# Reordering the first part and the loop of a planned attention and maxout kernel, and holding batch 3's loads behind w_out

## The chip, the cores and the metric

The kernel runs on one core of one Trainium2 chip. The metric is the device time of one execution in microseconds (us), as the median of several runs. All times below are us unless marked ns.

## The reference

`x` is 8 batches x 8 heads x 512 positions x 64, `state` 8 x 8 x 32 x 64. Per batch and head:

```
a     = softmax(x state^T / 8)          # 512 x 32
xread = a state                         # 512 x 64
a2    = softmax(state x^T / 8)          # 32 x 512
sread = a2 x                            # 32 x 64
```

The rows of `xread` and `sread` of a batch, heads side by side, are 544 rows of 512 numbers, 4352 rows in all. On each row `r` runs a maxout layer and an output layer:

```
h   = max(r w1, r w2, r w3)             # w1, w2, w3: 512 x 768
out = h w_out                           # w_out: 768 x 512
```

Inputs and output are float32.

## The kernel before

The kernel computes in bf16. GpSimd's (POOL's) DMAs convert on the way, so w1 to w3, w_out and nearly all of x come as bf16; the first half of batch 0's x and the states come as float32 over the queues of SyncE (SP) and ScalarE (ACT), and an engine casts them.

The products of `xread` with w1, w2 and w3 are not formed from `xread`. Since `xread = a state`, the kernel multiplies the states by the weights first: `G = state W` per batch (32 x 8 heads = 256 rows, 3 x 768 columns), and layer 1 is then `a G`, with only 256 instead of 512 terms to sum.

The whole work is a list of named steps in three texts, `FIRST` (lines 18 to 39: the loads, batches 0 and 1, the beginning of 2), `EACH` (lines 40 to 47: run five times, for batch b = 2 to 6, numbers in it are relative to b) and `LAST` (lines 48 to 64: batch 7, the `sread` rows of all batches, and the last stores). `perform` (line 543) calls the functions of the steps in the order of the text, and each engine and each queue then runs its own share strictly in that order, waiting where an operand isn't there. So the text is the schedule. Beside it stand `BANKS` and `PAIRS`: one digit for each request for a PSUM bank (four single banks, 0 to 3) or for a pair of banks (two pairs). A bank is written anew when its last holder has been copied out.

The steps, with the engine that does them; a last letter gives the engine or queue (D = VectorE or DVE, A = ACT, P = POOL, S = SP; two letters share the work in halves):

- `lst k`: load the states of batches 2k and 2k+1; `lxu`, `lxg b g`: load one half of batch b's heads (uncast over SP, cast over POOL); `lx b`: a whole batch over POOL; `lw m0 m1 i`: load columns m0*128 to m1*128 of w1, w2 or w3 (i = 0, 1, 2) over POOL; `lwo`: w_out over POOL. POOL has eight semaphores for its DMAs, and the ninth waits for the first to land.
- `cxu`: cast the half that came uncast. `stc k`, `stt k`, `stp k`: cast the states, turn them on TensorE (PE, line 221), place them as block matrices. `clr`, `zero`, `ident`, `xones`: constants. `warm`: load the exponential's table.
- `xt b g`, `xtc b g`: turn half of x on PE (line 236) and copy it out (line 243); `xtd b`: the same for a whole batch by a DMA transpose on SP (line 248).
- `sc`: scores on PE (line 261); `ex`: exponential on ACT (line 268); `sum`: row sums and their reciprocal on DVE (lines 275 and 277); `wt`: the product that gives `a` (line 283); `at`, `atc` or, by DMA on SP, `atd`: turn `a` (lines 294, 297, 301).
- `pad b`: POOL copies x with a column of ones beside it, 2 copies (line 310); `sr b`: `sread` on PE (line 326; for batches 0 and 1 straight from x, for the others from pad's copy); `srs`: divide it on DVE (lines 336 to 342); `srt`: turn it by a DMA on SP (line 345); `ap`: put it in place.
- `g b m`, `gc b m`: one slice of G, 128 columns of each of w1 to w3, on PE (line 362) and its copy (line 380); `gr b c0 c1`, `grc`: a run of columns of G (lines 362, 402, 405).
- `l1 b m`: layer 1 for 128 hidden columns, six matmuls into three banks (line 415); `m0`, `ma`, `mb`: the first bank is copied by ACT (line 430), DVE takes the maximum with the second (line 435) and the third (line 439).
- `l2 b j`: layer 2 for a quarter of the batch's rows, six matmuls (line 446); `l2c`: copy out (line 453); `so`: store (line 476).
- `busy n`: n matmuls on zeros (line 210) that fill PE where nothing is ready. `ones`: POOL sets a constant that only the last part reads (line 194).

In `FIRST` before, batches 0 and 1 go side by side: both softmaxes stand ahead of the first layer-1 step, POOL loads x of batch 1 first, then x of batch 0, then W in nine pieces of 128 to 384 columns, the last two behind batch 1's softmax products, then w_out and batch 3's x.

Of the kernel before, what the change touches and what calls it, by code (L numbers as in the profile page):

```python
# [15 lines left out]


FIRST = """
    lxu 0 0 S; lst 0 A; lxg 1 0; zero; warm; clr 0; clr 1; clr 2; clr 3; stc 0 D; ident; busy 1;
    lst 1 S; busy 2; busy 1; busy 2; busy 1; busy 1; stt 0; busy 1; busy 2; cxu 0 0 D; stp 0 AD;  # L20
    stc 1 A; lxg 0 1; xt 0 0; lxg 1 1; lw 0 1 0; busy 1; lw 0 3 1; xtc 0 0 A; xt 1 0; xones 0; busy 2;
    busy 1; lw 0 2 2; xtc 1 0 DA; sc 0 0; xt 0 1; lw 1 2 0; busy 1; busy 1; lw 2 4 0; lw 2 4 2; sc 1 0;
    ex 0 0; ex 1 0; busy 1; xtc 0 1 A; xt 1 1; busy 1; busy 1; sum 0 0; busy 1; stt 1; lw 3 6 1; busy 1;
    sc 0 1; busy 1; ex 0 1; xtc 1 1 D; busy 1; sc 1 1; ex 1 1; busy 1; stp 1 A; lxg 2 1; wt 0 0 P;
    busy 1; xones 1; at 0 0; sum 1 0; busy 1; busy 1; sum 0 1; sr 0; busy 1; sum 1 1; g 0 0; wt 1 0 P;
    g 1 0; gc 1 0 A; wt 0 1 D; sr 1; busy 1; srs 0; lxg 2 0; at 0 1; at 1 0; wt 1 1 P; atc 0 0 D;
    at 1 1; gc 0 0 D; atc 0 1 A; lw 4 6 2; srs 1; atc 1 0 A; g 1 1; atc 1 1 D; gc 1 1 A; g 0 1;
    l1 0 0 1; g 1 2; m0 0 0; g 0 2; l1 1 0; gc 0 1 D; gc 1 2 A; l1 1 1; m0 1 0; ma 0 0; mb 0 0; ma 1 0;
    lw 4 6 0; mb 1 0; l1 0 1; g 0 3; m0 1 1; g 1 3; gc 0 2 A; l1 0 2; ma 1 1; l1 1 2; xtd 2; pad 2;
    m0 0 1; mb 1 1; ma 0 1; m0 0 2; lst 3 A; gc 0 3 DA; l1 0 3; m0 1 2; lwo; gc 1 3 A; ones; g 0 5;  # L30
    g 1 4; mb 0 1; ma 0 2; lxg 3 0; m0 0 3; mb 0 2; gc 0 5 A; lst 2 S; ma 1 2; l1 1 3; stc 3 P; m0 1 3;
    l1 0 5; mb 1 2; g 0 4; gc 1 4 A; g 1 5; ma 0 3; l1 1 4; m0 0 5; gc 0 4 A; mb 0 3; ma 1 3; m0 1 4;
    lxg 3 1; l1 0 4; sc 2 -; gc 1 5 A; xtd 3; mb 1 3; gr 2 1024 1280; m0 0 4; gr 2 1280 1792; ex 2 -;
    grc 2 1280 1792 A; l1 1 5; m0 1 5; ma 0 5; stc 2 A; mb 0 5; gr 2 512 1024; gr 2 1792 2304; sr 2;
    ma 1 4; mb 1 4; ma 0 4; mb 0 4; l2 0 3; grc 2 512 1024 A; stt 2; grc 2 1024 1280 D; gr 2 0 512;
    l2 0 0; l2 0 1; l2 0 2; grc 2 1792 2304 A; sum 2 -; l2c 0 0 A; grc 2 0 512 A; ma 1 5; wt 2 - P;
    srs 2; l2c 0 3 A; stp 2 A; mb 1 5; l2c 0 2 D; atd 2; so 0 2 4 P; stt 3; l2c 0 1 A; stp 3 DA;
    so 0 0 2 A; lx 4;
# [638 lines left out]
```

## Time and profile before

| what | value |
|---|---|
| median of 3 runs | 153.15 (153.15 to 153.26) |
| the profiled execution | 153.01 |
| its span, first to last instruction | 151.2 |
| instructions | 3644 |
| HBM read, written | 15.20 MB, 8.91 MB |
| granted TensorE clock over the span | 0.999 of full |

The span is what the profile's times count from and to; 1.8 lie around it. The page gives busy time by engine, the chain of work that ended last, and groups of instructions by source line; the trace behind it can be asked for the instructions of one engine in order of time (start, duration, engine, line, operation, what is written and read, shapes, how many of the same kind in a row, and in brackets how long the engine stood idle before and what ended that), for single DMAs with the time from issue to landing, and for busy time in windows. Matmuls are pipelined, so the step from one start to the next is a matmul's price and its printed duration is longer.

### The profile page before, as it was taken

What the parts mean: (1) busy time and instruction counts of PE and PEld (TensorE: products, weight loads), DVE (VectorE), ACT (ScalarE), POOL (GpSimd) and SP (SyncE); (2) the same over time, 40 slices, a digit from 0 to 9 for tenths busy, and PEclk for the clock granted to TensorE, in tenths of its full rate; (3) what the DMA queues carried; (4) which work ended last, traced back from release to release, by engine and by line L of the source; (5) the groups of instructions that cost most, each with busy time, mean ns of one, the idle gap of its engine ahead of it and who ended that gap; (6) DMA issues with size and microseconds to landing.
All of it is one profiled execution on the core that took longest, in us unless ns stands there. A gap on an engine that the chain in (4) does not pass through costs nothing.

```text
span 151.2 us, 3644 instructions
## 1 busy us (share of the span) xinstructions
PE 146.6 (97%) x1434; PEld 73.6 (49%) x1434; DVE 115.1 (76%) x202; ACT 85.4 (56%) x147; POOL 54.7 (36%) x74
## 2 busy tenths in 40 slices
PE   6999999999999999999999999999999999999992
PEld 2465444344444443444354435443544445679771
DVE  6458899889168799879986998798879887675353
ACT  3567866779677671767175817581758353331220
POOL 6998518301336505460456054604260100001500
PEclk9999999999999999999999999999999999999999
DMA  3999999994919979998199829982133110300545
GB/s 112 241 193 195 198 196 203 161 197 59 204 53 262 225 89 269 152 193 182 60 168 228 174 94 163 206 176 80 72 139 87 68 79 7 131 8 17 188 170 198
DMA packets 38581, 22.30 MB, mean 147 GB/s; under 512 B 22032, under 2 KB 36368, under 8 KB 38560
## 3 DMA queue, kind: packets, MB, share of 16 engines
q0 software_dynamic: 15200, 13.44, 46.6%
q1 hardware_dynamic: 21920, 6.95, 23.5%
q10 hardware_dynamic: 1440, 1.64, 3.2%
q8 instruction: 12, 0.20, 0.5%
q14 instruction: 9, 0.07, 0.2%
HBM read 15.20 MB, written 8.91 MB: 159 GB/s over the span
## 4 chain that ended last, share of the span: by engine, by line
PE 92%; DMA 4%; issue 1%; POOL 1%; DVE 1%; POOLq 0%
PE pw L415 47%; PE po L446 25%; PE pg L362 6%; PE po L461 4%; DMA x<-in_x_dram 4%; PE psr L326 2%; PE ps L261 2%; PE idle L210 2%; PE pgh L362 1%; PE pat L294 1%; POOL x L169 1%; DVE held L521 0%; PE pt L221 0%; PE pxt L236 0%; PE idle L519 0%
## 5 line engine op out<-in xcount | busy, mean ns | idle before, releaser
L415 PE MATMUL pw<-aT,G 128*128 128x512 bf16 x288 | 66.6, 379 | 0.0
L430 ACT CAST t<-pw 128x512 bf16<-128x512 f32 (+1 forms) x54 | 30.4, 563 | 35.3 <-PE pw L415 21.6
L415 PEld LDWEIGHTS <-G 128*128 128x128 bf16 x288 | 27.2, 98 | 33.8 <-issue 2.4
L435 DVE TENSOR_TENSOR t<-t,pw 128x512 bf16<-128x512 bf16 (+1 forms) x54 | 35.3, 653 | 10.2 <-ACT t L430 7.7
L446 PE MATMUL po<-wout,ht 128*128 128x512 bf16 x168 | 39.8, 379 | 0.0
L439 DVE TENSOR_TENSOR ht<-t,pw 128x512 bf16<-128x512 bf16 x48 | 32.9, 685 | 4.1
L476 POOL DMA_DIRECT2D out_dram<-osb x12 | 6.9, 575 | 49.6 <-ACT t L430 20.4
L446 PEld LDWEIGHTS <-ht 128*128 128x128 bf16 x168 | 15.3, 98 | 19.2 <-issue 2.1
L283 POOL TENSOR_TENSOR a<-e,rden 128x1024 bf16<-128x1024 bf16 (+1 forms) x9 | 14.9, 1650 | 10.3 <-DVE rden L277 9.2
L402 ACT CAST G<-pg 128x1024 bf16<-128x1024 f32 (+1 forms) x19 | 17.1, 908 | 0.0
L310 POOL COPY xp<-x 128x1024 bf16<-128x1024 bf16 x12 | 12.3, 1065 | 5.0 <-DMA x<-in_x_dram 5.0
L453 DVE COPY osb<-po 128x512 f32<-128x512 f32 x14 | 9.6, 685 | 5.6 <-PE po L446 5.6
L453 ACT COPY osb<-po 128x512 f32<-128x512 f32 x15 | 8.9, 593 | 5.8 <-PE po L446 5.8
L210 PE MATMUL idle<-zero 128*128 128x512 bf16 x30 | 10.0, 436 | 1.3 <-DVE zero L188 1.3
L275 DVE TENSOR_REDUCE seen<-e 128x32 f32<-128x1024 bf16 (+1 forms) x10 | 10.0, 998 | 1.5 <-ACT e L268 1.5
L362 PE MATMUL pg<-w,bd 64*32 64x512 bf16 (+1 forms) x288 | 10.8, 362 | 0.0
L268 ACT ACTIVATE e<-ps 128x1024 bf16<-128x1024 f32 (+1 forms) x10 | 8.6, 861 | 2.1 <-PE ps L261 2.1
L402 DVE CAST G<-pg 128x1024 bf16<-128x1024 f32 (+1 forms) x10 | 9.5, 947 | 0.0
L471 POOL DMA_DIRECT2D out_dram<-osb x4 | 2.2, 542 | 19.9 <-ACT osb L465 19.9
L380 ACT CAST G<-pg 128x768 bf16<-128x768 f32 (+1 forms) x10 | 7.7, 774 | 2.1 <-PE pg L362 2.1
L415 PE MATMUL pw<-atp,w 128*128 128x256 bf16 x72 | 8.7, 272 | 0.0
L415 PEld LDWEIGHTS <-w 128*128 128x128 bf16 x72 | 6.9, 98 | 1.5
(71 smaller groups left out, 114.3 us busy)
## 6 DMA issues: line engine op xcount, KB each, us to landing
out_dram<-osb POOLq DMA_DIRECT2D x11, 512.0 KB, 3.1
x<-in_x_dram POOLq DMA_DIRECT2D x4, 512.0 KB, 6.6
x<-in_x_dram POOLq DMA_DIRECT2D x7, 256.0 KB, 8.4
w<-in_moe_w_dram POOLq DMA_DIRECT2D x5, 256.0 KB, 8.6
w<-in_moe_w_dram POOLq DMA_DIRECT2D x2, 384.0 KB, 8.8
wout<-in_moe_w_out_dram POOLq DMA_DIRECT2D x1, 768.0 KB, 9.5
out_dram<-osb SPq DMA_DIRECT2D x3, 256.0 KB, 2.3
osb<-in_x_dram SPq DMA_DIRECT2D x1, 512.0 KB, 4.0
```

Of the source, the lines that this page charges most:

```text
L210: nc.tensor.matmul(p, zero[:, 0:128], zero, start=True, stop=True)
L275: nc.vector.reduce_sum(out=den, in_=parity(e[b], g), axis=AX.X)
L283: times[c](out=parity(a[b], g).rearrange("p j g s n -> p j (g s) n"), in0=parity(e[b], g).rearrange("p j g s n -> p j (g s) n"), in1=rdens ...
L310: nc.gpsimd.tensor_copy(out=xp[b][:, :, :, g * (D + 1):g * (D + 1) + D], in_=v[:, g])
L362: nc.tensor.matmul(p(s, g), bd(b, 2 * s + g)[64 * g:64 * g + 64, g, :], f(w_sb[64 * g:64 * g + 64, s]), start=True, stop=True, tile_positi ...
L402: copier[c[g]](out=v[:, g:h], in_=p[:, g:h, 0:c1 - c0])
L415: nc.tensor.matmul(pw[i][:, 0:n], lhs(i, k), rhs(k), start=(k == 0), stop=(k == nk - 1))
L430: nc.scalar.copy(out=t0s[b, m][:, 0:n], in_=open_ps["l", b, m][0][:, 0:n])
L435: nc.vector.tensor_max(t1s[b, m][:, 0:n], t0s.pop((b, m))[:, 0:n], open_ps["l", b, m][1][:, 0:n])
L439: nc.vector.tensor_max(ht[b][:, m, :], t1s.pop((b, m))[:, 0:n], open_ps.pop(("l", b, m))[2][:, 0:n])
L446: nc.tensor.matmul(p, ht[b][:, m, j * 128:(j + 1) * 128], wout_sb[:, m, :], start=(m == 0), stop=(m == NM - 1))
L453: copier[c[i]](out=o[:, j, i * w:i * w + w], in_=p[:, i * w:i * w + w])
```

## The change

`FIRST` and `EACH` get new orders, `BANKS` and `PAIRS` are written anew to fit, `LAST` is untouched, and `set_ones` gets two lines.

- In `FIRST` batch 0 goes ahead alone: its x and the first 128 columns of each of w1 to w3 are loaded first, W then follows in 15 pieces, mostly of 128 columns, and batch 1's x between them. Batch 1's scores stand behind `l1 0 0`. Batch 0's and part of batch 1's softmax products go from POOL to DVE, some copies change their engine, state 1 is loaded by ACT behind `ex 1 1` and cast by POOL, state 2 is cast by POOL, and batch 0's first store goes to POOL. There are 29 fillers for 30. The order of layer 1 between batches 0 and 1, and the order of G's runs for batch 2, change too.
- `ones` now first copies one element of w_out on POOL, so it waits until w_out has landed; batch 3's two loads stand behind it.
- In `EACH` the transpose of the next x stands first, `sc` and `l2` 1 and 3 come before `l1 0`, the five runs of G come in another order, `sum` and `wt` come earlier, `l2c 0` goes from DVE to ACT, both stores stand at the end with the load of the next x between them, and `ap` is the last ACT step.

```diff
 FIRST = """
-    lxu 0 0 S; lst 0 A; lxg 1 0; zero; warm; clr 0; clr 1; clr 2; clr 3; stc 0 D; ident; busy 1;
-    lst 1 S; busy 2; busy 1; busy 2; busy 1; busy 1; stt 0; busy 1; busy 2; cxu 0 0 D; stp 0 AD;
-    stc 1 A; lxg 0 1; xt 0 0; lxg 1 1; lw 0 1 0; busy 1; lw 0 3 1; xtc 0 0 A; xt 1 0; xones 0; busy 2;
...
+    lst 0 A; lxu 0 0 S; zero; clr 0; clr 1; clr 2; clr 3; warm; lw 0 1 1; lxg 0 1; xones 0; busy 2;
+    busy 1; stc 0 D; ident; busy 3; busy 1; cxu 0 0 D; stt 0; busy 1; busy 1; lw 0 2 0; lw 0 1 2;
+    busy 1; xt 0 0; busy 1; busy 1; busy 1; busy 1; stp 0 A; xtc 0 0 D; lxg 1 0; xt 0 1; sc 0 0; busy 1;
+    busy 1; busy 1; busy 1; ex 0 0; xtc 0 1 D; sum 0 0; wt 0 0 D; lw 1 2 2; busy 2; sc 0 1; busy 1;
+    busy 1; busy 1; g 0 0; lw 1 2 1; g 1 0; busy 1; ex 0 1; at 0 0; sum 0 1; xones 1; wt 0 1 D; busy 2;
+    gc 0 0 A; atc 0 0 D; xt 1 0; xtc 1 0 A; busy 1; at 0 1; lxg 1 1; lw 2 3 2; busy 1; g 0 1; gc 1 0 A;
+    busy 1; atc 0 1 D; lw 2 3 0; lw 2 3 1; l1 0 0; sc 1 0; m0 0 0; gc 0 1 A; ma 0 0; xt 1 1; l1 0 1;
+    ex 1 0; g 0 2; mb 0 0; lw 3 4 2; sum 1 0; lw 3 4 1; xtc 1 1 A; sc 1 1; m0 0 1; wt 1 0 D; ex 1 1;
+    ma 0 1; lw 4 5 1; sr 0; g 1 1; gc 0 2 A; sum 1 1; sr 1; g 1 2; srs 1; srs 0; l1 0 2; mb 0 1; at 1 0;
+    lst 1 A; lw 3 4 0; lw 4 6 0; lw 4 6 2; gc 1 1 AD; atc 1 0 D; wt 1 1 P; at 1 1; g 0 3; lw 5 6 1;
+    atc 1 1 D; m0 0 2; g 1 3; gc 1 2 A; lxg 2 1; l1 1 0; l1 1 1; lxg 2 0; m0 1 0; l1 1 2; ma 0 2; g 0 5;
+    mb 0 2; gc 0 3 A; ma 1 0; mb 1 0; m0 1 1; stc 1 P; lwo; g 1 4; gc 1 3 A; l1 0 3; lst 3 A; ma 1 1;
+    m0 1 2; mb 1 1; stt 1; g 1 5; gc 0 5 A; g 0 4; l1 1 3; stc 3 P; xtd 2; ma 1 2; ones; lxg 3 0;
+    m0 0 3; gc 1 4 DA; lxg 3 1; stp 1 A; mb 1 2; l1 0 5; l1 1 4; m0 1 3; ma 0 3; mb 0 3; ma 1 3;
+    gr 2 1280 1792; m0 0 5; mb 1 3; gr 2 0 512; gc 0 4 A; lst 2 S; ma 0 5; gc 1 5 A; l1 0 4; mb 0 5;
+    stc 2 P; l1 1 5; m0 1 4; ma 1 4; mb 1 4; m0 0 4; ma 0 4; sc 2 -; grc 2 1280 1792 A; xtd 3; mb 0 4;
+    pad 2; m0 1 5; l2 0 0; l2 0 1; ma 1 5; ex 2 -; l2 0 3; sr 2; sum 2 -; l2c 0 0 A; gr 2 1024 1280;
+    gr 2 1792 2304; gr 2 512 1024; stt 2; l2 0 2; grc 2 0 512 A; mb 1 5; grc 2 1024 1280 D; l2c 0 1 A;
+    stp 2 D; stt 3; wt 2 - P; l2c 0 3 A; srs 2; grc 2 1792 2304 A; l2c 0 2 D; so 0 2 4 P; lx 4;
+    grc 2 512 1024 A; atd 2; so 0 0 2 P; stp 3 D;
 """
 EACH = """
-    gr 1 0 512; gr 1 1792 2304; l2 -1 0; grc 1 0 512 D; l1 0 0; pad 1; srt -2; m0 0 0; sc 1 -; l2 -1 1;
-    grc 1 1792 2304 A; ma 0 0; l2 -1 3; ex 1 -; gr 1 1024 1280; gr 1 512 1024; l2c -1 0 D;
-    gr 1 1280 1792; sr 1; l2c -1 1 A; so -1 0 2 P; mb 0 0; l1 0 1; grc 1 1024 1280 A; l2c -1 3 A; xtd 2;
-    m0 0 1; l1 0 2; m0 0 2; l1 0 3; sum 1 -; srs 1; grc 1 1280 1792 DA; ma 0 1; l1 0 5; mb 0 1; m0 0 3;
-    ma 0 2; ap -2 A; wt 1 - P; mb 0 2; m0 0 5; l2 -1 2; ma 0 3; grc 1 512 1024 A; mb 0 3; l1 0 4;
-    ma 0 5; mb 0 5; l2c -1 2 D; atd 1; m0 0 4; so -1 2 4 P; ma 0 4; lx 3; mb 0 4;
+    xtd 2; gr 1 1792 2304; pad 1; gr 1 0 512; l2 -1 1; grc 1 0 512 D; sc 1 -; grc 1 1792 2304 A; ex 1 -;
+    l2c -1 1 A; l2 -1 3; l1 0 0; l2 -1 0; l2c -1 3 A; gr 1 1280 1792; m0 0 0; sum 1 -; gr 1 1024 1280;
+    grc 1 1024 1280 A; ma 0 0; wt 1 - P; mb 0 0; l2c -1 0 A; gr 1 512 1024; sr 1; l1 0 1; srt -2;
+    m0 0 1; srs 1; l1 0 2; grc 1 1280 1792 DA; m0 0 2; l1 0 3; ma 0 1; m0 0 3; mb 0 1; ma 0 2; l1 0 5;
+    mb 0 2; m0 0 5; ma 0 3; l2 -1 2; grc 1 512 1024 A; l1 0 4; ma 0 5; mb 0 5; m0 0 4; mb 0 3;
+    l2c -1 2 D; so -1 2 4 P; lx 3; ma 0 4; mb 0 4; so -1 0 2 P; ap -2 A; atd 1;
 """
...
     def set_ones():
+        last = work.tile([128, 1], BF16, tag="last", bufs=1, name="last")
+        nc.gpsimd.tensor_copy(out=last, in_=wout_sb[:, 0, 0:1])
         nc.gpsimd.memset(ones, 1.0)
```

More of the change, by code (lines that the diff above doesn't have):

```diff
@@ L18 @@
 FIRST = """
-    lxu 0 0 S; lst 0 A; lxg 1 0; zero; warm; clr 0; clr 1; clr 2; clr 3; stc 0 D; ident; busy 1;
-    lst 1 S; busy 2; busy 1; busy 2; busy 1; busy 1; stt 0; busy 1; busy 2; cxu 0 0 D; stp 0 AD;
-    stc 1 A; lxg 0 1; xt 0 0; lxg 1 1; lw 0 1 0; busy 1; lw 0 3 1; xtc 0 0 A; xt 1 0; xones 0; busy 2;
-    busy 1; lw 0 2 2; xtc 1 0 DA; sc 0 0; xt 0 1; lw 1 2 0; busy 1; busy 1; lw 2 4 0; lw 2 4 2; sc 1 0;
-    ex 0 0; ex 1 0; busy 1; xtc 0 1 A; xt 1 1; busy 1; busy 1; sum 0 0; busy 1; stt 1; lw 3 6 1; busy 1;
@@ L24 @@
[L24 to L38, printed above, removed]
+    lst 0 A; lxu 0 0 S; zero; clr 0; clr 1; clr 2; clr 3; warm; lw 0 1 1; lxg 0 1; xones 0; busy 2;
@@ L66 @@
 BANKS = """
[3 rows of a table removed]
[3 rows of a table added]
 """
 PAIRS = """
-    0110101010 1010101010 1001010010 1001010010 10
+    0101010101 0110110101 0101010101 0101010101 01
 """
```

6 rows, old and new, of the table BANKS are left out of this document.

## The prediction

> **What bounds the kernel now.** I read the page's shares first, then the chain of waits, then TensorE (PE) in order of time, then the windows of the loop. The forecast is a difference of small terms, so most rows here are prices.
>
> ```profile
> PE 146.6 (97%) x1434; PEld 73.6 (49%) x1434; DVE 115.1 (76%) x202; ACT 85.4 (56%) x147; POOL 54.7 (36%) x74
> ...
> L210 PE MATMUL idle<-zero 128*128 128x512 bf16 x30 | 10.0, 436 | 1.3 <-DVE zero L188 1.3
> ```
>
> PE is occupied for 97% of the span, but 30 of its matmuls are fillers ("idle") that compute nothing. Real work can't be saved: both plans do the same. So the question is how much PE time is filler or waiting. The window of one loop pass of five:
>
> ```profile
> 73.38:88.63 15.25, 15.25 (x149) 6.81 (x148) 12.80 (x21) 8.86 (x15) 6.04 (x7) 1.00 0.81 159
> ```
>
> Columns: window, length, then busy time of PE, weight loads, DVE, ACT, POOL. This pass takes 15.25 and PE fills it; the clock is granted in full (1.00). No order of the loop can gain much there. What is left is the first part. The chain of waits and the timeline of all engines say what holds it:
>
> ```profile
> 3.58 5.97 DMA x<-in_x_dram
> ```
> ```profile
> 5.65 0.62 PE L236 MATMUL pxt<-ident,x 128*128 128x128 bf16 x8 [0.20 <-DVE x L177]
> ...
> 6.62 0.45 PEld L236 LDWEIGHTS <-x 128*128 128x128 bf16 x8 [0.47 <-DMA x<-in_x_dram]
> ```
>
> PE waits for x: the first software-queue load (256 KB as stored) is there at 6.6, the third (768 KB together) at 9.55. So the queue brings 512 KB in 2.95, or 0.575 per 100 KB, and the order of loads decides what PE can start. Unit prices on PE are the steps from one start to the next:
>
> ```profile
> 9.60 0.62 PE L236 MATMUL pxt<-ident,x 128*128 128x128 bf16 x8
> 10.06 0.81 PE L210 MATMUL idle<-zero 128*128 128x512 bf16 x3
> 10.71 0.38 PE L221 MATMUL pt<-ident,st 128*128 128x128 bf16 x4
> ...
> 11.14 0.40 PE L261 MATMUL ps<-bd,xT 128*128 128x64 bf16 x8
> 11.38 0.60 PE L210 MATMUL idle<-zero 128*128 128x512 bf16 x2
> ...
> 12.48 0.38 PE L294 MATMUL pat<-ident,a 128*128 128x128 bf16 x4
> 12.70 0.59 PE L210 MATMUL idle<-zero 128*128 128x512 bf16 x2
> 13.22 0.63 PE L326 MATMUL psr<-x,e 128*32 128x128 bf16 x32
> 13.79 0.39 PE L210 MATMUL idle<-zero 128*128 128x512 bf16 x1
> 14.11 0.52 PE L362 MATMUL pg<-w,bd 64*32 64x384 bf16 x16
> 14.55 0.63 PE L326 MATMUL psr<-x,e 128*32 128x128 bf16 x32
> ...
> 16.56 1.47 PE L415 MATMUL pw<-aT,G 128*128 128x512 bf16 x6
> ...
> 18.41 4.12 PE L415 MATMUL pw<-aT,G 128*128 128x512 bf16 x18
> 22.46 0.52 PE L362 MATMUL pg<-w,bd 64*32 64x384 bf16 x16
> ...
> 36.31 0.45 PE L326 MATMUL psr<-xp,e 128*32 128x65 bf16 x32
> 36.70 1.47 PE L446 MATMUL po<-wout,ht 128*128 128x512 bf16 x6
> ```
>
> Hence: xt 0.46, a filler 0.217, sc 0.24, at 0.22 (and stt, four like matmuls, the same), sr 0.57, two g 0.44. A filler followed by g takes 0.32, so going over to g costs 0.10 (a switch). 18 layer-1 matmuls take 4.05 with one switch, so a group l1 of six takes 1.30.
>
> **The change, part by part.**
>
> *Up to the first layer-1 group.* Before, `l1 0 0` starts at 16.56. After: `xt 0 0` still starts at 5.65, since its cast waits for the same SyncE load; one slow filler less ahead of it (seven for eight) is worth nothing. `xt 0 1` then needs the first W slice and x's second half, 128 + 256 = 384 KB of the software queue: 6.6 + 128 x 0.00575 = 7.35. Four fillers would let PE go at 5.65 + 0.46 + 0.87 = 6.98, so it waits 0.37. From there the plan is xt, sc, six fillers, sc, three, switch, g, g, one, at, two, xt, one, at, one, switch, g, one: 2 x 0.46 + 2 x 0.24 + 2 x 0.22 + 3 x 0.22 + 15 x 0.217 + 2 x 0.10 = 5.96. `l1 0 0` starts at 13.3. The other loads are in time by the same rate: W's first slices (768 KB) at 9.6 against `g 0 0` at 10.3; `lxg 1 0` (1,024 KB) at 11.0 against 11.6; the second slices (1,280 KB) at 12.5 against 12.8.
> This isn't 3.3 gained. Before had done more by its 16.56: stt 1, one xt, two sc, two at, two sr, one g = 0.22 + 0.46 + 0.48 + 0.44 + 1.14 + 0.22 = 2.96. So the gain is 16.56 - 13.3 - 2.96 = **0.3**.
>
> *From there to layer 2.* VectorE (DVE) now has batch 0's maxima and batch 1's softmax at once:
>
> ```profile
> 13.10 0.63 DVE L275 TENSOR_REDUCE seen<-e 128x16 f32<-128x512 bf16 x1
> ...
> 13.93 0.63 DVE L283 TENSOR_TENSOR a<-e,rden 128x512 bf16<-128x512 bf16 x1
> 14.47 0.16 DVE L339 RECIPROCAL seen<-psr 128x2 f32<-128x2 f32 x1
> ...
> 14.87 0.41 DVE L297 COPY aT<-pat 128x512 bf16<-128x512 bf16 x1
> ...
> 23.09 0.55 DVE L380 CAST G<-pg 128x384 bf16<-128x384 f32 x1
> ...
> 24.17 0.69 DVE L435 TENSOR_TENSOR t<-t,pw 128x512 bf16<-128x512 bf16 x1
> ...
> 25.58 0.69 DVE L435 TENSOR_TENSOR t<-t,pw 128x512 bf16<-128x512 bf16 x1
> ```
>
> From start to start, ma with mb takes 1.41, a sum with its reciprocal 0.83, wt 0.54, srs 0.40, half a gc 0.46, atc 0.34. The twelve pieces between `l1 0 0` and `l1 1 0` on DVE (two of ma and mb, of sum, srs and atc; one wt, one half gc) make 7.0, and they begin when ACT's first copy of `l1 0 0` ends, about 1.2 after 13.3. So `l1 1 0`, which needs the last atc, comes at 21.5, while PE's own work up to it (three l1, two sc, xt, five g, two sr, two at) is 7.5: waits of 0.7, two switches included. Nine more l1, four g, stt 1, two gr and `sc 2` are 13.8; DVE needs 1.41 per l1 against 1.30 + 0.1 on PE, so I allow four switches and 0.05, 0.45 in all. Layer 2 starts at 13.3 + 21.3 + 1.15 = 35.75. Before starts it at 36.70 having done `gr 2 1024` and one more 512-column run (0.4 by the 0.22 of a g of 384 columns) and `sr 2` (0.39) besides: 35.75 + 0.8 = 36.5, **0.2 ahead**. Third W slices (1,920 KB) arrive at 16.2 by the rate; `g 0 2` wants them at 16.7 (13.3, two l1, sc, xt, a switch). A rate one tenth lower makes them 0.2 late, two tenths 0.8: bounds 0 and 0.8, and I take 0.1.
>
> A slice of 128 columns writes rows of 256 bytes; 12 of the 15 W loads are now such, before 2 of 9. The trace has one right behind a load of twice its size, issued 0.74 earlier, and both took 7.6 from issue to landing:
>
> ```profile
> w<-in_moe_w_dram POOLq DMA_DIRECT2D x1, 256.0 KB, 7.6
> ```
> ```profile
> w<-in_moe_w_dram POOLq DMA_DIRECT2D x1, 128.0 KB, 7.6
> ```
>
> So 128 KB landed 0.74 later, 0.58 per 100 KB: full rate, and I add nothing. [...]
>
> *The wait in front of batch 3's x, and POOL's line.* The copy of one element costs POOL a small operation, 0.2 as a bound. What counts is what queues behind it: `lxg 3 0`, `lxg 3 1`, `stc 2`, `pad 2`, `wt 2`. PE's `sr 2` waits for pad 2, SyncE's `xtd 3` for x. SyncE itself now has `xtd 2` ahead of state 2's load.
>
> ```profile
> wout<-in_moe_w_out_dram POOLq DMA_DIRECT2D x1, 768.0 KB, 9.5
> xT<-x SPq DMA_TRANSPOSE x1, 8.1
> ```
> ```profile
> x<-in_x_dram POOLq DMA_DIRECT2D x1, 256.0 KB, 9.9
> stf<-in_state_dram SPq DMA_DIRECT2D x1, 128.0 KB, 6.8
> ```
> ```profile
> 14.17 1.29 POOL L283 TENSOR_TENSOR a<-e,rden 128x512 bf16<-128x512 bf16 x1 [0.40 <-DVE rden L277]
> ...
> 22.11 2.05 POOL L310 COPY xp<-x 128x1024 bf16<-128x1024 bf16 x2 [4.97 <-DMA x<-in_x_dram]
> 24.09 0.82 POOL L185 DMA_DIRECT2D wout<-in_moe_w_out_dram  x1
> ```
>
> `sum 1 1` ends at 19.0 in the DVE line, `wt 1 1` on POOL at 20.3; three loads at 0.8 and `stc 1` (half the elements of one of pad's two copies: 0.5) put w_out's issue at 23.2 and its landing, at 9.5, at 32.7; it is needed at 35.75. Batch 3's loads are out by 34.5, state 2 cast by 35, pad 2 done by 37.3. `sr 2` comes three l2 after 35.75, at 39.7. Cover: 2.4. Batch 2's x lands near 26.4 (640 KB at the rate behind 22.7) and its transpose, at 8.1, at 34.5 for `sc 2` at 35.2: 0.7. Batch 3's x lands near 37.5 (512 KB); its transpose took 4.3 in a quiet queue:
>
> ```profile
> xT<-x SPq DMA_TRANSPOSE x1, 4.3
> ```
>
> So 41.8, for `sc 3` at 44.4 (35.75, five l2, sr, the gr runs, two stt, two switches); at 9.9 and 8.1 it would be 51.7. I price the wait at 0, with 7.3 as its far end. It can't gain: `sr 2` at 36.31 shows no idle time in front of it, so no transfer holds it now.
>
> *The loop.* The same pieces and the same two switches per pass. `sc` comes one l2 group earlier and needs ACT's cast of the 1792 run, 1.0 long, within 1.3; `l2c 0` goes from DVE to ACT, which has slack (8.9 of 15.25). 0 to 0.1 per pass; I take 0.1 for all five. `wt` and pad come earlier on POOL, both stores late, with the next x's load between them: that load keeps its place behind the second store, so `xtd` still starts as before. In the first part `so 0 0 2` goes from ACT to POOL and holds `pad 3` by one issue. The last part is the same text with other bank numbers: 0.
>
> Sum: -0.2 + 0.1 + 0.1 = 0. The profiled execution is 153.01 (span 151.2 and 1.8 around it); the median of the runs is 153.15. I forecast 153.1.
>
> **Rivals.**
>
> *Faster:* the waits of 1.15 shrink to the six switches, because ACT and DVE overlap neighbouring instructions more than I allow: 0.5 gained, 152.6. For it: in 18.41 to 22.46 before hardly waits at all. Against it: the DVE line of 7.0 has no gap in which to overlap.
>
> *Slower, the POOL line:* pad 2 ends after 39.7, and PE, in order, holds the rest of layer 2 behind `sr 2`. Its trigger is state 1: ACT issues that load only behind `ex 1 1`, at about 18; at 6.8 it lands at 24.8 instead of the 22.7 that I need, POOL's `stc 1` waits, and w_out lands at 34.8. State 2, behind batch 2's transpose, adds as much. It decides when the two slips pass 2.4 together. Before, pad 2 was done at 24.2, twelve ahead of its use; that cover is gone. A slip of 1.5 beyond it gives 154.6. Against it: with w_out issued at once, there is less beside it in the queue.
>
> [...]
>
> *The read doesn't act:* w_out may be there before POOL, held by state 3's cast, reaches the read. Then x 3 comes earlier and nothing on the path changes: 153.1, part of the forecast.
>
> **Chances.** No change, 152.8 to 153.6: 0.42. Faster: 0.28. POOL line: 0.21. Slices: 0.03. Waits I have not seen, slower: 0.06. A measurement of this kernel can tell about 0.2%, 0.3 us, from no change. The forecast's own range lies 0.32 within that, 0.04 below, 0.06 above. So faster 0.31 (0.27 + 0.04), same 0.33 (0.32 + 0.01), slower 0.36. Range 152.3 to 154.6: out of it are the slices, half of the unseen waits, the longer slips and the ends of the faster case.
>
> **What would show it.** `l1 0 0` near 13.3 and the first layer-2 matmul near 35.75; a PE wait of 0.3 to 0.4 ahead of `xt 0 1`; DVE without idle time from 14.5 to 21.5; pad 2 ending before 39; passes of 15.25 to 15.3. Wrong if POOL's w_out load lands after 35, if `sc 2` or `sr 2` starts with idle time in front of it, or if a pass is over 15.4.

## The result and the profile after

The changed kernel takes 154.81 (median of 4 runs, 154.40 to 155.74) beside 153.20 (153.15 to 153.32): a ratio of 1.010, 95% interval 1.007 to 1.013. A second series gave 154.59 (9 runs, 153.33 to 155.16), ratio 1.008 (1.005 to 1.010). So the change loses 1.3 to 1.6, where I forecast no change. Each ratio, here and below, leaves out the runs that took over 1.5% longer than the quickest run of the same kernel, while medians and ranges keep them. The profiled execution took 154.52, its span 152.7 against 151.2.

PE of the changed kernel in order of time (start, duration, and in brackets the idle time in front and what ended it; all lines of code stand 2 further down than before):

```profile
4.66 1.49 PE L212 MATMUL idle<-zero 128*128 128x512 bf16 x3
5.94 0.85 PE L238 MATMUL pxt<-ident,x 128*128 128x128 bf16 x8
...
13.42 0.36 PE L364 MATMUL pg<-w,bd 64*32 64x384 bf16 x8 [0.21 <-DMA w<-in_moe_w_dram]
13.71 0.39 PE L212 MATMUL idle<-zero 128*128 128x512 bf16 x1
13.94 1.46 PE L417 MATMUL pw<-aT,G 128*128 128x512 bf16 x6
...
36.65 0.64 PE L263 MATMUL ps<-bd,xT 128*128 128x64 bf16 x16 [0.35 <-DMA xT<-x]
37.13 4.05 PE L448 MATMUL po<-wout,ht 128*128 128x512 bf16 x18
41.11 0.45 PE L328 MATMUL psr<-xp,e 128*32 128x65 bf16 x32
```

`l1 0 0` starts at 13.94 instead of 13.3: with the 2.96 that it still has to do, it is 0.34 behind before's 16.56. `g 0 1` waits for W, `sc 2` for batch 2's transpose; layer 2 starts at 37.13 instead of 35.75. `sr 2` has no idle time in front. The first row is worth a look too: three fillers take 1.28 (4.66 to 5.94), 0.43 each for the 0.217 of the prediction, twice as long, which I read as half the clock. The trace records the full clock from 6.43 on, that of the kernel before from 4.16 on.

The chain of waits between 6 and 37 names what held PE (start, duration, what):

```profile
6.70 6.59 DMA w<-in_moe_w_dram
13.29 0.14 issue
13.42 0.36 PE pg L364 x8
...
19.91 1.05 POOL a L285
20.96 0.75 POOL w L180
21.71 0.73 POOL x L169
22.44 5.33 DMA x<-in_x_dram
...
27.86 8.75 DMA xT<-x
36.61 0.05 issue
36.65 0.64 PE ps L263 x16
```

Read from its end: the scores of batch 2 start at 36.65, its transpose took from 27.86 to 36.61, the second half of its x was issued at 22.44 and landed at 27.77. It was issued so late because POOL had first to do `wt 1 1` (19.91) and to issue the last W slice. Meanwhile the queue ran nearly dry: all DMA engines together moved 26 to 64 GB/s between 21.8 and 22.6, and 192 to 256 in the 0.7 before that drop began.

The passes of the loop (window, length, PE, weight loads, DVE, ACT, POOL, clock, DMA):

```profile
44.00:59.28 15.28, 15.28 (x150) 6.91 (x149) 13.30 (x23) 9.04 (x16) 6.02 (x7) 1.00 0.76 147
59.28:74.86 15.58, 15.44 (x151) 6.82 (x150) 12.13 (x20) 9.52 (x17) 6.04 (x7) 1.00 0.86 172
74.86:90.14 15.28, 15.28 (x150) 6.82 (x149) 12.12 (x20) 9.41 (x17) 6.04 (x7) 1.00 0.78 158
```

The loop starts 1.13 late (44.00 for 42.87), one pass loses 0.33 against the 15.25 of before, the other four 0.03 each: 1.6 in all, beside the 1.5 between the spans. For the long pass the chain shows ACT, which stands in `ap` (its last step of a pass now) until `srt` lands, and only then casts the run of G that the next scores need:

```profile
57.73 2.31 DMA ats<-sr
60.04 0.02 issue
60.06 0.48 ACT atp L352
60.55 0.86 ACT G L404
61.40 0.04 issue
61.45 0.57 PE ps L263 x14
```

### The profile page after: what moved, and what is told of

Read it like the earlier page. It is cut to its first block, busy times and chain, and to the rows that moved or that the text cites. A ratio compares the mean times of both kernels' runs of the same rounds, so it can differ in the third digit from the quotient of the medians.

```text
span 152.7 us, 3640 instructions
## 1 busy us (share of the span) xinstructions
PE 147.6 (97%) x1433; PEld 74.4 (49%) x1433; DVE 114.4 (75%) x202; ACT 85.6 (56%) x147; POOL 58.5 (38%) x82
## 4 chain that ended last, share of the span: by engine, by line
PE 71%; DMA 15%; POOL 5%; DVE 4%; issue 2%; ACT 2%; POOLq 0%; DVEq 0%; SPq 0%
PE pw L417 35%; PE po L448 23%; DMA xT<-x 6%; PE po L463 4%; DMA w<-in_moe_w_dram 4%; PE pg L364 4%; DMA x<-in_x_dram 3%; POOL w L180 2%; PE ps L263 2%; POOL x L169 2%; DMA ats<-sr 2%; PE psr L328 1%; DVE t L437 1%; DVE seen L277 1%; ACT t L432 1%
## 5 line engine op out<-in xcount | busy, mean ns | idle before, releaser
L448 PE MATMUL po<-wout,ht 128*128 128x512 bf16 x168 | 40.6, 379 | 0.0
L441 DVE TENSOR_TENSOR ht<-t,pw 128x512 bf16<-128x512 bf16 x48 | 32.4, 684 | 3.9
L478 POOL DMA_DIRECT2D out_dram<-osb x13 | 7.5, 575 | 45.7 <-ACT atp L352 33.8
L285 POOL TENSOR_TENSOR a<-e,rden 128x1024 bf16<-128x1024 bf16 (+1 forms) x7 | 12.5, 1785 | 8.3 <-DVE seen L341 3.5
L455 ACT COPY osb<-po 128x512 f32<-128x512 f32 x20 | 11.3, 594 | 4.2 <-PE po L448 4.2
L180 POOL DMA_DIRECT2D w<-in_moe_w_dram x15 | 11.4, 768 | 2.4 <-DMA x<-in_x_dram 1.2
L312 POOL COPY xp<-x 128x1024 bf16<-128x1024 bf16 x12 | 12.3, 1060 | 0.0
L364 PE MATMUL pg<-w,bd 64*32 64x512 bf16 (+1 forms) x288 | 11.5, 364 | 0.5 <-issue 0.2
L382 ACT CAST G<-pg 128x768 bf16<-128x768 f32 (+1 forms) x12 | 8.8, 752 | 1.2 <-PE pg L364 1.2
L473 POOL DMA_DIRECT2D out_dram<-osb x4 | 2.2, 544 | 19.0 <-ACT osb L467 19.0
L407 ACT CAST G<-pgh 128x256 bf16<-128x256 f32 x10 | 3.2, 375 | 9.1 <-PE pgh L364 9.1
```

Of the source, the lines that this page charges most:

```text
L180: nc.gpsimd.dma_start(out=w_sb[:, :, i, m0 * 128:m1 * 128], in_=(moe_w1, moe_w2, moe_w3)[i].rearrange("(kk p) f -> p kk f", p=128)[:, :, m ...
L285: times[c](out=parity(a[b], g).rearrange("p j g s n -> p j (g s) n"), in0=parity(e[b], g).rearrange("p j g s n -> p j (g s) n"), in1=rdens ...
L312: nc.gpsimd.tensor_copy(out=xp[b][:, :, :, g * (D + 1):g * (D + 1) + D], in_=v[:, g])
L364: nc.tensor.matmul(p(s, g), bd(b, 2 * s + g)[64 * g:64 * g + 64, g, :], f(w_sb[64 * g:64 * g + 64, s]), start=True, stop=True, tile_positi ...
L441: nc.vector.tensor_max(ht[b][:, m, :], t1s.pop((b, m))[:, 0:n], open_ps.pop(("l", b, m))[2][:, 0:n])
L448: nc.tensor.matmul(p, ht[b][:, m, j * 128:(j + 1) * 128], wout_sb[:, m, :], start=(m == 0), stop=(m == NM - 1))
```

## The experiments

All times are medians beside the kernel before on the same chip (153.3 to 153.4 in each series).

| kernel | time (lowest to highest, runs) | ratio (95%) |
|---|---|---|
| changed kernel again | 154.59 (153.33 to 155.16, 9) | 1.008 (1.005 to 1.010) |
| `srt` first | 154.61 (153.79 to 155.72, 7) | 1.009 (1.006 to 1.012) |
| x 2 early | 153.69 (153.50 to 154.44, 12) | 1.003 (1.001 to 1.004) |
| one filler more | 154.56 (153.88 to 155.35, 7) | 1.008 (1.005 to 1.011) |
| both: x 2 early, `srt` first | 153.47 (152.86 to 153.71, 6) | 1.000 (0.998 to 1.002) |
| both, unit matrix first | 154.23 (153.96 to 158.00, 6) | 1.006 (1.004 to 1.008) |
| without the read | 159.83 (156.36 to 160.58, 4) | none given |
| new loop alone | 154.26 (154.04 to 154.59, 6) | 1.006 (1.004 to 1.007) |
| w_out held behind x 2 | 159.23 (158.37 to 162.55, 6) | 1.037 (1.033 to 1.040) |
| new first part with x 2 early, old loop | 157.17 (156.33 to 157.53, 6) | 1.023 (1.020 to 1.027) |
| both, x first | 153.25 (152.61 to 153.56, 6) | 0.998 (0.995 to 1.001) |
| both, without the read | 155.00 (153.49 to 160.63, 6) | 1.007 (1.002 to 1.011) |
| both, x first, W in pairs | 153.64 (153.11 to 156.02, 12) | 1.003 (1.001 to 1.005) |
| both, x first, again | 153.01 (152.77 to 154.03, 12) | 0.999 (0.998 to 1.001) |

And what their traces show, one profiled execution each: the time from which the clock is full, the landing of the third load of the software queue and of the second W slices, the start of `l1 0 0`, the landing of batch 2's transpose, the idle time in front of `sc 2`, the first layer-2 matmul.

| kernel | clock | third load | second W | `l1 0 0` | transpose | idle | layer 2 |
|---|---|---|---|---|---|---|---|
| changed | 6.43 | 9.75 | 13.29 | 13.94 | 36.61 | 0.35 | 37.13 |
| again | 7.20 | 9.43 | 12.99 | 13.89 | 36.98 | 0.54 | 37.50 |
| `srt` first | 4.00 | 9.41 | 12.95 | 13.60 | 36.90 | 1.06 | 37.42 |
| one filler more | 5.86 | 9.67 | 13.32 | 13.97 | 36.88 | 0.46 | 37.41 |
| x 2 early | 7.02 | 9.25 | 12.90 | 13.79 | 35.29 | 0 | 36.51 |
| both | 4.79 | 8.77 | 12.30 | 13.11 | 32.99 | 0 | 35.66 |
| both, unit matrix first | 5.90 | 10.28 | 13.81 | 14.46 | 35.20 | 0 | 37.05 |
| both, x first | 4.64 | 8.57 | 12.69 | 13.34 | 34.08 | 0 | 35.89 |
| both, x first, again | 5.10 | 8.66 | 12.21 | 13.08 | 33.74 | 0 | 35.60 |

**The changed kernel again.** No edit.

> The changed kernel once more, unaltered. Theory: its loss of about 1.5 is made of four waits in fixed places: 0.3 in front of `l1 0 0` (it starts at 13.9 because the second W slice lands at 13.3), 0.4 to 0.5 in front of `sc 2` (batch 2's transpose lands at 36.6), 0.3 in front of the scores at the start of the second loop pass (61.45 instead of 61.13), and 0.1 to 0.2 spread over the passes. Then a second trace shows the same places, each within 0.2, and a time of 154.4 to 155.7. Rival: the first profile was one of several courses, because the order in which packets of different queues are served is left to chance; then at least one of these four differs by over 0.5.

Its waits of PE (line, what it waited for: us in total, times, longest):

```profile
PE ps L263 <- DMA xT<-x: 0.5, 1, 0.5
PE pg L364 <- DMA w<-in_moe_w_dram: 0.4, 1, 0.4
```

The waits for W and for the transpose are there again, but W's now stands in front of `g 0 2`, and `l1 0 0` starts 0.90 behind the second W slice instead of 0.65. The long pass isn't there: all passes take 15.28. Of the other traces with `srt` in its old place one has it once more, at 15.43 (x 2 early). So that 0.3 comes and goes, while the wait for the transpose is there in every trace with x 2 late.

**`srt` first.**

```diff
 EACH = """
-    xtd 2; gr 1 1792 2304; pad 1; gr 1 0 512; l2 -1 1; grc 1 0 512 D; sc 1 -; grc 1 1792 2304 A; ex 1 -;
+    srt -2; xtd 2; gr 1 1792 2304; pad 1; gr 1 0 512; l2 -1 1; grc 1 0 512 D; sc 1 -; grc 1 1792 2304 A; ex 1 -;
...
-    grc 1 1024 1280 A; ma 0 0; wt 1 - P; mb 0 0; l2c -1 0 A; gr 1 512 1024; sr 1; l1 0 1; srt -2;
+    grc 1 1024 1280 A; ma 0 0; wt 1 - P; mb 0 0; l2c -1 0 A; gr 1 512 1024; sr 1; l1 0 1;
```

> Only `srt` is moved, ahead of the transpose of x on SyncE's queue in each pass. Theory: the second pass begins 0.3 late because ACT stands in `ap`, its last step of the first pass, until `srt` lands (60.04), and `srt` stands behind the transpose of x 4, which starts only when x 4 has landed at 54.6; with `srt` first, `ap` is over in time, the second pass takes 15.28 like the others instead of 15.58, and the time falls by 0.3. Rival: the transpose of the second batch's `a`, the bank hand-over or the cast of the run of G decides as well; then the pass stays at 15.5 to 15.6 and nothing is gained.

Its passes take 15.28, as those of the last trace did without it, and the median doesn't move: without the other wait removed, there was nothing to gain in it. By chance this run had the full clock at 4.00, and shows something else:

```profile
13.08 0.36 PE L363 MATMUL pg<-w,bd 64*32 64x384 bf16 x8 [0.21 <-DMA w<-in_moe_w_dram]
...
36.95 0.64 PE L262 MATMUL ps<-bd,xT 128*128 128x64 bf16 x16 [1.06 <-DMA xT<-x]
```

It is 0.34 ahead of the changed kernel at `g 0 1` and 0.30 behind it at `sc 2`: here the transpose takes back what the first part gains.

**x 2 early.** The last W slice and x 2 are issued while POOL would stand waiting for `wt 1 1`'s sums:

```diff
-    lst 1 A; lw 3 4 0; lw 4 6 0; lw 4 6 2; gc 1 1 AD; atc 1 0 D; wt 1 1 P; at 1 1; g 0 3; lw 5 6 1;
-    atc 1 1 D; m0 0 2; g 1 3; gc 1 2 A; lxg 2 1; l1 1 0; l1 1 1; lxg 2 0; m0 1 0; l1 1 2; ma 0 2; g 0 5;
+    lst 1 A; lw 3 4 0; lw 4 6 0; lw 4 6 2; lw 5 6 1; lxg 2 1; lxg 2 0; gc 1 1 AD; atc 1 0 D; wt 1 1 P;
+    at 1 1; g 0 3; atc 1 1 D; m0 0 2; g 1 3; gc 1 2 A; l1 1 0; l1 1 1; m0 1 0; l1 1 2; ma 0 2; g 0 5;
```

> Only the order on GpSimd: the last W slice and both halves of batch 2's x are issued ahead of `wt 1 1`, where GpSimd stands idle from 16.4 to 19.9, instead of behind it. Theory: x 2 then lands at 25.0 to 25.5 instead of 27.8, its transpose starts before w_out's packets do and lands at 33.2 to 34.0 instead of 36.6; `sc 2` starts without idle time at about 36.2, and the time falls by 0.4 to 0.5. Rival: the transpose is served only when w_out is through (33.1), however early it is issued; then it lands at 36 to 36.6 as now and nothing is gained.

```profile
17.66 1.48 POOL L168 DMA_DIRECT2D x<-in_x_dram  x2 [0.87 <-DMA w<-in_moe_w_dram]
20.00 1.05 POOL L284 TENSOR_TENSOR a<-e,rden 128x512 bf16<-128x512 bf16 x1 [0.86 <-ACT G L381]
```
```profile
36.04 0.63 PE L262 MATMUL ps<-bd,xT 128*128 128x64 bf16 x16
```

x 2 is issued at 17.66 instead of 21.71, and `wt 1 1` is hardly later for it (20.00 for 19.91). The queue doesn't run dry in front of x 2, which lands at 26.79 instead of 27.77. `sc 2` starts without idle time; the transpose lands at 35.29, later than I expected but in time. The median falls by 0.9, and the spread from 1.8 to 0.9. That is more than the 0.4 to 0.5 that I had forecast; layer 2 starts 0.62 to 0.99 earlier than in the four traces above with x 2 late. The edit issues the last W slice earlier too, but PE waits for that slice in neither trace. This is the largest part of the loss.

**One filler more** (`busy 3` becomes `busy 4` ahead of `stt 0`).

> Only one filler more, so that eight instead of seven run before the turn of the states. Theory: the eighth brings the full clock at about 4.2 again instead of 6.4, `xt 0 0` starts at 5.65 instead of 5.94, but `l1 0 0` still starts at 13.9, since it is the second W slice at 13.3 that holds `g 0 1`: the time stays within 0.15. Rival: the late clock is itself the 0.3 that the first part loses; then `l1 0 0` comes at 13.6 and the time falls by 0.3.

With eight fillers the full clock comes at 5.86, not at 4.2: its moment isn't set by the eighth filler. `l1 0 0` (13.97) and the time stay. My theory was wrong about the clock and right about W.

**Both steps.** x 2 early and `srt` first in one kernel.

> Both single steps together: batch 2's x issued ahead of `wt 1 1`, and `srt` first on SyncE's queue in the loop. Theory: `sc 2` starts at 36.0 without idle time, and the second pass, which took 15.44 with the x step alone and 15.28 with the `srt` step alone, takes 15.28: a span of 151.8 to 151.9, a time of 153.5 to 153.6, which is 0.2 to 0.4 above the kernel before. What is left over the kernel before is then 0.5 to 0.6 in front of layer 2 and 0.03 in each pass. Rival: the slow second pass in two of five traces was chance and has no part in the median; then the time equals that of the x step alone, 153.7.

```profile
12.60 0.36 PE L362 MATMUL pg<-w,bd 64*32 64x384 bf16 x8
12.89 0.39 PE L210 MATMUL idle<-zero 128*128 128x512 bf16 x1
13.11 1.24 PE L415 MATMUL pw<-aT,G 128*128 128x512 bf16 x5
```
```profile
35.19 0.63 PE L261 MATMUL ps<-bd,xT 128*128 128x64 bf16 x16
35.66 4.05 PE L446 MATMUL po<-wout,ht 128*128 128x512 bf16 x18
```

All passes take 15.28, and the time is that of the kernel before. The trace is of the quickest of the six runs (152.86). In it W came early (second slices at 12.30, forecast 12.5), and with it the two milestones of the prediction: 13.11 for 13.3, 35.66 for 35.75. Its span is 150.9, 0.3 under before's.

**Unit matrix first.** `ident` moves ahead of the first load, `xones 0` to `xones 1`.

> On top of the last one: GpSimd makes the unit matrix ahead of its first load instead of between the second and the third, and sets the ones of x 0 later, so that the third load (W) is issued at 3.05 instead of 3.65, if the unit matrix fits into the 0.9 that GpSimd stands idle at the start. Theory: the queue ran short of issued loads; at 0.74 to 0.75 for an issue and 0.73 for its 128 KB it never makes up for the gap of 0.6, and each W slice lands that much later. Then the second W slices land at 12.3 to 12.5 instead of 12.9 to 13.3, `l1 0 0` starts at 13.3 to 13.5, and the time falls by 0.2 to 0.4 against the last one. Rival: the queue moves what it can from the first load on, and the order of the issues is nothing; then the second W slices land at 12.9 to 13.3 as in all five traces so far, and the time stays (or rises by up to 0.5, if the unit matrix delays the first load).

```profile
8.15 0.62 PE L236 MATMUL pxt<-ident,x 128*128 128x128 bf16 x8 [0.63 <-DMA x<-in_x_dram]
```

My theory of a queue that ran short of issues at the start finds no support. The first load is issued 0.2 later (1.56 for 1.37) and lands 0.8 to 1.1 later (6.72 for 5.60 to 5.96 in the other traces with W first); the third is issued 0.4 earlier (3.22 for 3.65) and still lands later than in any other trace (10.28), 2.2 behind the second load. `g 0 1` comes at 13.94, 0.20 behind its turn for W, and the time rises by 0.8 against the last kernel. The late first load stands in the same run, so this doesn't test the order of the issues by itself.

**Without the read** (the two new lines of `set_ones` are left out).

> The changed kernel without the read of w_out, so that batch 3's x is issued at about 30.2, behind state 3's cast, instead of 33.5. Theory: the read does act, and it holds x 3's 512 KB back from the transpose of x 2, which already waits for w_out; without it `xT` of batch 2 lands 1 to 2.5 later than 36.6 to 37.0, `sc 2` waits 1.5 to 3, and the time rises by 1 to 2. Rival: transposes and x 3 share the engines, and nothing or little (under 0.3) changes at `sc 2`; x 3 and its transpose come 2 to 3 earlier, which nothing waits for.

```profile
40.57 0.64 PE L261 MATMUL ps<-bd,xT 128*128 128x64 bf16 x16 [4.49 <-DMA xT<-x]
```
```profile
41.12:44.53 3.41, 3.41 (x13) 1.23 (x9) 2.12 (x3) 1.77 (x3) 3.08 (x5) 0.50 0.65 123
```

x 3 is issued at 29.57, and the transpose of x 2 lands at 40.52, 12.7 after its issue. PE stands for 4.49, and then the clock falls to half for 3.41. The trace is of a run of 159.87; the others took 156.36, 159.78 and 160.58. Even beside the quickest of the four the read, which I had priced at nothing, is worth 1.8 in this plan (156.36 for 154.59). What the other three lose beyond that I don't price.

**The new loop alone**, behind the old first part.

> The kernel before with the new loop alone (the first part, and the code without the read, are those of before; the bank digits of the loop are renamed to fit). Theory: the new loop costs 0.02 to 0.03 a pass, 0.1 to 0.15 in all, and its first pass perhaps 0.3 where `srt` comes late: 153.4 to 153.7 where before is 153.2 to 153.3, so that nearly all of the loss lies in the first part. Rival: the loop carries a half of the loss and more, over the five passes: 154 or above.

```profile
45.89 0.63 PE L261 MATMUL ps<-bd,xT 128*128 128x64 bf16 x16 [0.84 <-ACT G L402]
```

The passes after the first take 15.26 to 15.28. But the old first part leaves ACT with other work at the seam, and the first scores of the new loop wait 0.84 for it. This wait isn't in the changed kernel, so the run doesn't measure the loop's share of the median, although its time is one that the rival forecast (154 or above); it agrees with 0.03 a pass at most.

**w_out held behind x 2.** POOL reads an element of x 2 ahead of issuing w_out:

```diff
     def load_wout():
+        here = work.tile([128, 2], BF16, tag="here", bufs=1, name="here")
+        nc.gpsimd.tensor_copy(out=here, in_=x_sb[2][:, 255:257])
         nc.gpsimd.dma_start(out=wout_sb, in_=moe_w_out.rearrange("(kk p) f -> p kk f", p=128))
```

> The changed kernel, with one thing more: GpSimd reads one element of each half of batch 2's x before it issues w_out's load, so that w_out (issued at 23.7 so far, while x 2 lands at 27.8) goes out only when x 2 is there, at about 28, together with the transpose of x 2. x 2 itself stays late. Theory: it is not x 2's lateness alone that costs, but w_out's 768 KB, which stand in the software queue ahead of the transpose and are served first; with w_out behind, the transpose lands at 32.2 to 34 instead of 36.6 to 37.0, `sc 2` starts without idle time at 36.2 to 36.5, w_out lands at 34 to 36, before layer 2 at 36.7, and the time falls by 0.4 to 0.9, as with x 2 early. Rival: the transpose is slow of itself whenever a load runs beside it (8.1 in the kernel before); then it lands at 36 as now, `sc 2` still waits, or layer 2 waits for w_out, and the time is as now or longer.

```profile
36.65 0.64 PE L265 MATMUL ps<-bd,xT 128*128 128x64 bf16 x16 [0.32 <-DMA xT<-x]
39.47 4.06 PE L450 MATMUL po<-wout,ht 128*128 128x512 bf16 x17 [2.18 <-DMA wout<-in_moe_w_out_dram]
```

The rival is right about the time, if not about the cause. The two were issued together (28.07 and 28.59). The transpose's 2048 data packets of 256 bytes start between 29.36 and 32.49, w_out's from 32.11 on. Yet the transpose's landing is signalled only at 36.60, while w_out's packets run, 8.5 after its issue; w_out took 10.8. (The trace is of the longest of the six runs, 162.55, so its other waits aren't those of the median.)

In the changed kernel the order is the other way round. Here are its two queues from 28 to 31, from 31 to 33 and from 33 to 34.5 (packets, MB, share of 16 engines; q0 carries the loads, q1 the transpose):

```profile
q0 software_dynamic: 481, 0.49, 111.3%
...
q1 hardware_dynamic: 571, 0.15, 68.6%
q0 software_dynamic: 208, 0.20, 59.5%
...
q1 hardware_dynamic: 1501, 0.38, 116.9%
```

The first stretch has no packet of the transpose, the last none of w_out, and between them w_out ends while the transpose begins: its first data packet starts at 31.33, 3.47 behind its issue, where that of x 3's transpose starts 1.18 behind its own (40.53 and 39.35). So with w_out in the queue the transpose takes 6.8 to 9.8 in these traces, whichever of them goes first (4.3 without it, for x 3 of the changed kernel). Of the two steps that I tried on this wait, x 2 early is the one that helps.

**The new first part with x 2 early, and the old loop.**

> The new first part with batch 2's x issued early, and the loop of before (bank digits of the loop renamed to fit). Theory: every pass takes 15.25 to 15.26 instead of 15.28, 0.1 to 0.15 in all; if the seam between the two plans fits, the time is 153.3 to 153.5. Rival: as where the new loop follows the old first part (0.84 of idle time at the first `sc` of the loop, for an ACT cast), the seam itself costs more than the passes give; then 153.8 to 154.5, and the two halves of the plan are only good together.

```profile
46.66 1.46 PE L416 MATMUL pw<-aT,G 128*128 128x512 bf16 x6 [0.98 <-DMA aT<-a]
```

The old passes take 15.25, but the old loop wants the turned `a` of batch 2 before it has landed: it is 1.9 later than before at the last scores (108.97 for 107.04). Another 2.7 lie behind the last store (landed 152.04, span 155.7; before 150.24 and 151.2). In that time DVE stands: its next instruction starts 2.83 after its last branch, in the kernel before 0.49; why stays open. As they stand, the two halves of the plan fit only each other.

**Both, x first.** `lw 0 1 1; lxg 0 1;` becomes `lxg 0 1; lw 0 1 1;`. It ran twice.

> On top of the two steps together (x 2 early, `srt` first): x's second half is loaded ahead of W's first slice. Theory: what holds `l1 0 0` is the second W slice plus 0.65 whenever that lands after 12.6, so the earlier `xt 0 1` (its half lands at 6.6 instead of 7.0 to 7.7) is worth 0 to 0.2 there, and the time stays at 153.3 to 153.6. Rival: the softmax of batch 0 is the longest chain in all runs and starts 0.5 earlier; then `l1 0 0` comes at 12.6 to 12.9 whatever W does, and the time falls by 0.3 to 0.5, below the kernel before.

> The same kernel as with x first, unaltered, beside the one with pairs. Theory: 153.0 to 153.5, the same as the kernel before within 0.2%, with no idle time at `sc 2` and the third load landing at 8.5 to 8.8. Rival: its time of 153.25 was luck of the first 10 us; then the third load lands at 9.3 or later, `l1 0 0` starts at 13.6 or later, and the median is 153.6 or more.

The third load lands at 8.57 and 8.66, with W first at 8.77 to 10.28 in eleven traces. That speaks for the order of the first two loads, though two traces, with only 0.11 to the nearest of the others, don't settle it. `l1 0 0` comes at 13.34 (0.65 behind the second W slice, so W still holds it) and 13.08, between what the two expected. The time is within 0.2% of the kernel before, at best level with it.

**Both, without the read.**

> The two steps together, without the read of w_out. Theory: batch 3's x then goes out at about 27 behind w_out, and its 512 KB too are served ahead of the transpose of x 2, which in the run with the read landed 2.2 after w_out; it lands at 36 to 38 instead of 33, `sc 2` waits 1 to 2.5, and the time rises by 1 to 2.5. Rival: since x 2 comes 1.7 earlier than in the changed kernel, its transpose is through before x 3's packets begin, and the read is worth nothing here (within 0.3).

```profile
39.30 0.73 PE L259 MATMUL ps<-bd,xT 128*128 128x64 bf16 x16 [3.21 <-DMA xT<-x]
```

x 2 is issued early here and the transpose, issued at 26.92 beside w_out and x 3, lands at 39.26. The clock falls again behind the wait, to half from 39.70 to 43.11. The trace is of a run of 158.55, one of the two longest of six; by the ratios (1.007 for 1.000) the read is worth about 1.0 here.

**Both, x first, W in pairs.** `lw 0 1 1`, `lw 1 2 1` become `lw 0 2 1`; `lw 0 1 2`, `lw 1 2 2` become `lw 0 2 2`.

> On top of x first, x 2 early and `srt` first: the first two slices of each of w1 to w3 come as one load of 256 columns (rows of 512 bytes), three loads for five, and the same bytes ahead of `g 0 1`. Theory: a slice with rows of 256 bytes takes 0.735 per 128 KB in all traces and one with rows of 512 or 768 bytes 0.66 to 0.67, and two issues are saved; with pairs all six slices are in the core by 10.5 to 11.0, `g 0 0` waits 0.2 to 0.5 but `g 0 1` never does, and `l1 0 0` starts at 12.9 to 13.3 (13.1 and 13.3 in the two runs before it); from there 0.1 to 0.4 come from the rest of W landing earlier: 152.9 to 153.2. Rival: it is chance in the first 10 us (the third load has landed between 8.6 and 9.8) and not the size of the rows; then `g 0 0`, which waits for more bytes, takes what `g 0 1` gains, and the time is 153.2 to 153.6.

```profile
10.73 0.52 PE L362 MATMUL pg<-w,bd 64*32 64x384 bf16 x16 [0.29 <-DMA w<-in_moe_w_dram]
```

All six slices are there at 10.60, `g 0 1` waits for nothing, and `l1 0 0` is no earlier (13.79): `g 0 0` waited for more bytes (0.29), with the clock late too (6.28). The median is 0.6 above that of x first in the same series. The rival's reading holds. The price of the rows can be read from the landings: in the changed kernel slices of 128 KB land 0.73 to 0.74 apart (11.82, 12.56, 13.29), the pairs of 256 KB 1.33 and 1.29 apart (7.98, 9.31, 10.60), so 0.73 against 0.65 for 128 KB.

## Why the prediction was wrong

**The step that failed** is the cover at `sc 2`: batch 2's x "near 26.4", its transpose "at 34.5 for `sc 2` at 35.2: 0.7". x 2 landed at 27.77 and the transpose took 8.75, so it came 2.1 late; in the four traces with x 2 late and the read in place it landed at 36.6 to 37.0. For x 2 I had let the queue run without a gap behind 22.7, though by my own line three issues stand behind `wt 1 1` on POOL, and ahead of them it ran nearly dry. With x 2 early x 2 lands at 26.79, still 0.4 behind my 26.4, and 0.9 of the 1.3 lost in the median are gone. With `srt` first as well the time is level with before. That step alone moved nothing, and the intervals of x 2 early and of both steps overlap, so which part the last 0.2 to 0.4 belongs to stays open.

For the transpose I had taken 8.1 as the price beside w_out, without asking for the order of the packets. That 8.75 came out near it is chance. In the kernel before, the transpose's data packets start between 23.44 and 26.57, ahead of w_out's (from 26.72 on), and only the landing is late, at 30.23. In the changed kernel they stand behind w_out's, which start from 26.69 to 32.77, so `sc 2` hung on w_out's end, and the earlier `l1 0 0` of the run with `srt` first gained nothing. x 2 early keeps that order, but w_out's last packet starts at 32.04 there and the transpose lands 1.3 earlier.

**W's arrival** comes second. I priced the queue by before's, which starts with x; started with a W slice, the third load lands at 8.8 to 10.3 where my rate gives 8.8. In eight of the thirteen traces with this first part and W in single slices, `l1 0 0` starts 0.65 after the second W slice (13.94 and 13.29, 13.60 and 12.95 in the table); in the other five 0.81 to 0.90. In the changed kernel W is the 0.64 that `l1 0 0` comes late. Where x went first, `l1 0 0` came at 13.08 and 13.34, and at 13.79 with W in pairs. Whether a W slice at the head slows the queue, and why, stays open, and no run has W on time with x 2 late.

**Rows of 256 bytes**, which I put at "full rate", took a tenth more than rows of 512 bytes, by the landings: 0.73 in the changed kernel for 0.65 with W in pairs, per 128 KB. It hurt no term: my sum priced 128 KB at 0.74. The chance of 0.03 for the slices rests on a much higher price for them, which no run shows: what the runs showed is 0.73 for 0.65.

**The first gain of 0.3 and the sum of -0.2 at layer 2** were right where their conditions held: with x 2 early and W on time, `l1 0 0` came at 13.11 and 13.08 and layer 2 at 35.66 and 35.60, which with the 0.8 that before had done more is 0.24 and 0.30 ahead of before. Both traces are of quick runs (152.86 and 152.79, medians 153.47 and 153.01); the median gains less. From `l1 0 0` to layer 2 I had 22.45; they took 22.55 and 22.52. DVE's line (`l1 1 0` 8.33 behind `l1 0 0`, forecast 8.2) was right too.

**One slow filler less** I put as "worth nothing", and one filler more changed nothing, but not for my reason. `xt 0 0` didn't wait for its cast: the slow fillers in front of it made it start at 5.94 for 5.65. When the clock becomes full doesn't go by the number of fillers, and where it is late, the wait for W hides most of it (`l1 0 0` 0.89 to 0.90 behind the second W slice instead of 0.65 in the three traces where the clock came last, at 6.98 to 7.20).

**The POOL line**, my slower rival, gave nearly the measured time by another mechanism: state 1 landed at 23.05, not after 24.8, w_out at 33.14 for 32.7, and `sr 2` never waited. `pad 2` ended at 39.49 for my 37.3, still 1.6 ahead of `sr 2`, because PE was late as well.

**The read** I had priced at 0 because "no transfer holds it now", said of `sr 2` before. That looked at x 3's users alone. It holds 512 KB back from x 2's transpose, and leaving it out costs 1.8 or more in the changed kernel and about 1.0 with both steps: the change as a whole loses in spite of it.

**The loop**: 0.1 forecast in all, 0.03 a pass measured, and in some executions 0.15 to 0.3 more in the second pass, in the changed kernel's trace by `srt`, a wait that I hadn't looked for.

Of the signs that I had named, DVE's line and w_out's landing before 35 came; `l1 0 0`, layer 2 and `pad 2` came late, `xt 0 1` at 7.49 didn't wait (the slow fillers in front of it filled the time). Of the signs that I had said would prove me wrong, two came: idle time in front of `sc 2`, and a pass over 15.4 (15.58).

What stays: the version with both steps and x first, run twice, is level with the kernel before (0.998 and 0.999, both intervals hold 1), and no version beats it for certain.

## What to carry to other kernels

Batch 2's transpose hung on three things in a row: POOL's issue of x 2, x 2's landing, and the transfer itself. The cover of such a chain is what is left of three small margins. Work out the issue time from what stands ahead of it on its queue, and move issues ahead of a compute step for which the issuing engine only waits.

Price a transfer by the packets beside it and their order, not by its own duration in another plan (x 3's transpose took 4.3 in the changed kernel, x 2's 8.75, and 6.8 to 9.8 in the traces with w_out in the queue), and ask of each wait in a queue what it keeps out of the way of others. An experiment on an earlier stage shows nothing in the time as long as a later wait takes its gain (with `srt` first, 0.34 ahead at `g 0 1` and 0.30 behind at `sc 2`); remove that wait first.
